# Softmax threshold and denominators as short sums on VectorE, and q and k loaded between their predecessors' copies

## The chip, the cores and the metric

The kernel runs on one core of a Trainium2 chip, in one launch. The metric is the device time of that core in microseconds (us). The core has TensorE (PE for the matmuls, PEld for its weight loads), VectorE (DVE), ScalarE (ACT), GpSimd (POOL) and SyncE (SP), which here issues nearly all DMAs.

## The reference

```python
def _attn_ref(q, k, v, tau):                  # q, k, v: 4 x 8 x 576 x 64, float32
    scores = scale * np.matmul(q, k.transpose(0, 1, 3, 2))
    thresh = np.max(scores, axis=-1, keepdims=True) - tau
    scores = np.where(scores >= thresh, scores, -1000000000.0)
    scores = scores - np.max(scores, axis=-1, keepdims=True)
    attn = np.exp(scores)
    attn = attn / (np.sum(attn, axis=-1, keepdims=True) + 1e-09)
    return np.matmul(attn, v)

def reference(...):
    x = attention(q, k, v, tau)               # to 2304 tokens x 512
    x = moe(x)     # a bias by modality, the best of 8 experts, relu between two matmuls, times the gate
    return moe2(x) # x @ w_in, h * tanh(softplus(h)), @ w_out
```

## The kernel before

The program has three stages one after the other on TensorE: attention (until about 347 us of the span), the 8 experts, and the dense last layer. The change is in the first.

**Attention.** Two heads of one batch element make a pair: 16 pairs. A pair's 576 rows of q are five units of 128 rows (the fifth has 64 rows of either head together). Below, unit (i, j) is unit j of pair i. `unit(u)` writes out one step of a pipeline by hand: scores of unit u, transposes of unit u - 1's probabilities, and products with v for unit u - 2. The order of instructions on each engine is that of the code; engines wait for one another by semaphores.

For each head x of a unit: `score` makes 128 x 576 negated scores in PSUM (tile `s`; two such tiles exist, so that the scores of a head wait until the tile's last user, two heads back, is done with it); `red` (L373, DVE) takes their minimum `mn`; `expo` has the threshold `th` = `mn` + `taus` made by a small instruction (L379, on POOL, in the first two units on DVE), and the exponential `e` (L381, ACT, with `mn` as its bias); `keep` (L391, DVE) sets to zero what lies beyond `th`, writes the probabilities `p`, and sums them into a column of the pair's 128 x 9 tile `rs`. `keep` is the tile `s`'s last user. At the end of unit (i, 1), `inverse` (L450 and L451, DVE) turns the denominators of the pair before into their reciprocals: plus 1e-9, then a reciprocal.

**q and k of the next pair.** In units 0 and 1 of a pair, `Prep` transposes q and k of the next one on TensorE: four transposes of `mq` or `mk` (L275) between the scores of the first and of the second head, and one of the last rows `rq` or `rk` (L291) later. ACT copies the results into `raw`, POOL splits `raw` into a high and a low part (`hi`, `lo` for q, `hik`, `lok` for k; L314 and L323), and SP copies the parts by DMA into the layouts that the scores read: `xq` (four DMAs of 128 KB, L332) and `xkh`, `xkl` (four DMAs each of 144 KB, L310). POOL's work on q stands in unit 1, that on k in unit 2. `Prep`'s own data is loaded a pair ahead: at the end of unit (i, 2), `load_qk` and `load_v` issue the loads of pair i + 2: `mq` and `mk` (256 KB each, in pieces of 256 bytes), `rq` and `rk` (64 KB each; of their 128 rows the first 64 are there too in `mq` and `mk`, and not used), and v. Further work (clearing `y_d`, the gate of the experts with stores to `x_d`, first expert weights) share the engines and the DMA queue in some pairs.

Of the kernel before, what the change touches and what calls it, by code (L numbers as in the profile page):

```python
# [9 lines left out]
F32 = mybir.dt.float32  # L10
# [10 lines left out]
P = 128  # L21
B, H, S, D = 4, 8, 576, 64
# [13 lines left out]
HK = S // 2  # L36
# [50 lines left out]
def chain_kernel(ctx: ExitStack, tc: tile.TileContext, q, k, v, tau, mid, w_gate, mbias, w1, w2, w_in, w_out, cst, out):  # L87
    nc = tc.nc
    ctx.enter_context(tc.manual_schedule())

    def pool(stack, name, bufs, **kw):
        return stack.enter_context(tc.tile_pool(name=name, bufs=bufs, reuse_waits="tile", **kw))
# [13 lines left out]
    def pa_tile(name):  # L106
        return ps_a.tile([P, 512], F32, tag="a", name=name)
# [23 lines left out]
    st_p = pool(ta, "st", 8)  # L131
# [6 lines left out]
    tau_b = att.tile([P, 1], F32, name="tau_b")  # L138
# [13 lines left out]
    PAIRS = [(b, g) for b in range(B) for g in range(NP)]  # L152
    ld = {}
    opd = {}
    res = {}

    def load_qk(i, n):
        b, g = PAIRS[i]
        h0 = 2 * g
        nm, src = (("q", q), ("k", k))[n]  # L160
        m = ld_p.tile([P, 4, 2, D], F32, name=f"m{nm}")
        r = ld_p.tile([P, 2, D], F32, name=f"r{nm}")
        ld[i, nm] = (m, r)
        parts = [
            lambda: nc.sync.dma_start(out=m, in_=src[b, h0:h0 + 2, 0:512, :].rearrange("h (p t) d -> p t h d", t=4)),
            lambda: nc.sync.dma_start(out=r, in_=src[b, h0:h0 + 2, 448:576, :].rearrange("h p d -> p h d"))]
        if i > 0:
            for x in parts:
                x()
        return parts  # L170

    def load_v(i):
        b, g = PAIRS[i]
# [6 lines left out]
        nc.sync.dma_start(out=vb[64:128, 128:192], in_=v[b, h0, 512:576, :])  # L180
        ld[i, "v"] = (m, vb)

    first = dict(zip("qk", (load_qk(0, 0), load_qk(0, 1))))
    first["i"] = [lambda: nc.sync.dma_start(out=ident, in_=cst[:, 0:P])]
    first["t"] = [lambda: nc.sync.dma_start(out=tau_b, in_=tau.to_broadcast([P, 1]))]
    for x in FIRST.split():
        first[x[0]][int(x[1:] or 0)]()
    load_qk(1, 0)
    load_qk(1, 1)

    neg = att.tile([P, 1], F32, name="neg")
    qsc = att.tile([P, 1], F32, name="qsc")
    taus = att.tile([P, 1], F32, name="taus")
# [153 lines left out]
    def score(i, j, x):  # L347
        o = opd[i]
        assert o["wait"] == 0 or i == 0 and j < NRAW
        s = ps_s.tile([P, 2, 512], F32, tag="s", name="s")  # L350
        res[i, j, x] = {"s": s}
        h = slice(64 * x, 64 * x + 64)
        for c in range(2):
            ks = slice(c * HK, (c + 1) * HK)
            kh = slice(k_off(x) + c * HK, k_off(x) + (c + 1) * HK)
            d = s[:, c, 0:HK]
            if i == 0 and j < NRAW:
                nc.tensor.matmul(d, lhsT=o["rawq"][h, 128 * j:128 * j + 128], rhs=o["rawk"][h, kh], start=True, stop=True)
            elif j < 4:
                qa = o["xq"][:, x, 128 * j:128 * j + 128]  # L360
                nc.tensor.matmul(d, lhsT=qa, rhs=o["xkh"][:, x, ks], start=True, stop=False)  # L361
                nc.tensor.matmul(d, lhsT=qa, rhs=o["xkl"][:, x, ks], start=False, stop=True)  # L362
            else:
                nc.tensor.matmul(d, lhsT=o["xm"][:, 0, :], rhs=o["hik"][:, kh], start=True, stop=False)
                nc.tensor.matmul(d, lhsT=o["xm"][:, 0, :], rhs=o["lok"][:, kh], start=False, stop=False)
                nc.tensor.matmul(d, lhsT=o["xm"][:, 1, :], rhs=o["hik"][:, kh], start=False, stop=True)

    def red(i, j, x):
        r = res[i, j, x]
        if x == 0:  # L370
            r["mn"], r["th"] = st_p.tile([P, 2], F32, name="mn"), st_p.tile([P, 2], F32, name="th")
        mn = res[i, j, 0]["mn"]
        nc.vector.tensor_reduce(out=mn[:, x:x + 1], in_=r["s"][:, :, 0:HK], op=ALU.min, axis=AX.XY)  # L373

    def expo(i, j, x):
        r = res[i, j, x]
        r["e"] = e_p.tile([P, 2, HK], F32, name="e")
        mt = res[i, j, 0]
        (nc.vector if (i, j) < (0, 2) else nc.gpsimd).tensor_scalar(  # L379
            out=mt["th"][:, x:x + 1], in0=mt["mn"][:, x:x + 1], scalar1=taus[:, 0:1], scalar2=0.0, op0=ALU.add, op1=ALU.add)  # L380
        nc.scalar.activation(out=r["e"], in_=r["s"][:, :, 0:HK], func=AF.Exp, scale=-1.0, bias=res[i, j, 0]["mn"][:, x:x + 1])  # L381

    def keep(i, j, x):
        r = res[i, j, x]
        if (j, x) == (0, 0):
            opd[i]["rs"] = rs_p.tile([P, 9], F32, name="rs")
        rs = opd[i]["rs"]
        if x == 0:
            r["pp"] = pp_p.tile([P, 2 * S], F32, name="p")
        p = res[i, j, 0]["pp"][:, x * S:(x + 1) * S].rearrange("p (a b) -> p a b", a=2)  # L390
        nc.vector.scalar_tensor_tensor(  # L391
            out=p, in0=r["s"][:, :, 0:HK], scalar=res[i, j, 0]["th"][:, x:x + 1], in1=r["e"],
            op0=ALU.is_le, op1=ALU.mult, accum_out=rs[:, 2 * j + x:2 * j + x + 1])
        r["p"] = res[i, j, 0]["pp"][:, x * (S + 64):x * (S + 64) + 512]

    def turn(i, j, x, cols):
# [49 lines left out]
        nc.scalar.copy(out=opd[b, "xt"][:, g, j * P:j * P + n], in_=a[:, 0:n])  # L446

    def inverse(i):
        rs = opd[i]["rs"]
        nc.vector.tensor_scalar(out=rs, in0=rs, scalar1=1e-9, scalar2=None, op0=ALU.add)  # L450
        nc.vector.reciprocal(out=rs, in_=rs)  # L451

    class Back(Piece):
# [573 lines left out]
    def unit(u):  # L1027
        i, j, n = at(u)
        i1, j1, n1 = at(u - 1)
        i2, j2, n2 = at(u - 2)  # L1030
        x, taken = None, False
        if n > 0 and j < 2 and i + 1 < len(PAIRS):
            x = Prep(i + 1, j)
        elif j == 3 and u >= 8:
            x = Back(u // 5 - 1)
        elif n > 0 and bg and hasattr(bg[0], "pe") and bg[0].ready():
            x, taken = bg.pop(0), True
        if n > 0:
# [59 lines left out]
    for n in PREP0:  # L1098
        x = Prep(0, n)
# [402 lines left out]
    with tc.If(cnt > i0):  # L1502
# [24 lines left out]
        with tc.For_i(b0, NT // 256) as k_:  # L1527
# [4 lines left out]
                out=y[1][:, :, 0:256].bitcast(F32),  # L1532
                in_=y_d.rearrange("k p (a c) -> k p a c", c=256)[:, :, bass.ds(k_, 1), :].rearrange("k p a c -> p k (a c)"))
# [60 lines left out]
```

## Time and profile before

| | |
|---|---|
| time before, median of 3 runs | 992.59 us (992.57 to 993.57) |
| time of the profiled execution | 996.13 us |
| its span, first to last instruction | 994.3 us |
| mean granted TensorE clock | 0.988 of full |
| busy in the span: PE, PEld, DVE, ACT, POOL | 94%, 79%, 82%, 52%, 67% |
| L373, minimum, DVE | 144 times, 750 ns |
| L391, `keep`, DVE | 144 times, 815 ns |
| L379, threshold, POOL | 140 times, 290 ns |
| `mq`, `mk`; `rq`, `rk` loads | 16 times each, 256 KB; 64 KB |

All times are microseconds from the span's start, durations of one instruction are nanoseconds where marked. The busy shares are means over three stages with different limits, so that a stage is read from its own windows and waits. A wait shown behind a row is the time in which that row's engine was idle before it, with what is taken to have ended it.

### The profile page before, as it was taken

Reading aid. Unit: us, or ns where it says so; the run is one execution under the profiler, and the core shown is the slowest. Engines: PE = TensorE matmul, PEld = TensorE weight load, DVE = VectorE, ACT = ScalarE, POOL = GpSimd, SP = SyncE. Lnnn points to the kernel's source line nnn. Section 1 sums busy time; section 2 is a strip of 40 time slices with the busy share of each in tenths; the row PEclk is TensorE's granted clock in tenths of the full one; section 3 lists DMA queues with packets and bytes.
Section 4 is the critical chain, followed back from the end, with each engine's and each line's share of the span. In section 5 each row is a group of like instructions: output and inputs, shape, how many; then the busy total and the mean of one; then the engine's idle time right before and its main releaser. Section 6 shows DMA issues by size and latency. Waiting matters only on the chain. (4 is left out here: it accounts for less than half of the span.)

```text
span 994.3 us, 17630 instructions
## 1 busy us (share of the span) xinstructions
PE 930.9 (94%) x6157; PEld 783.2 (79%) x6157; DVE 815.8 (82%) x1116; ACT 519.7 (52%) x1044; POOL 665.5 (67%) x771
## 2 busy tenths in 40 slices
PE   8899989998979997899999799999999999999994
PEld 5788888788868776688887788888888888888983
DVE  5677786687957768978876579999999999999992
ACT  4577777776768732366654643434344333433341
POOL 4354564455556364577876786887887888787883
PEclk9899999999999999999999999999999999999998
DMA  7678766646567053498899849010001100000000
GB/s 173 138 176 232 190 174 154 143 116 153 136 165 171 7 181 96 134 333 264 257 323 314 292 165 335 1 43 22 22 1 43 43 1 22 11 33 1 1 32 34
DMA packets 120526, 127.47 MB, mean 128 GB/s; under 512 B 54576, under 2 KB 83504, under 8 KB 119920
## 3 DMA queue, kind: packets, MB, share of 16 engines
q1 hardware_dynamic: 117472, 116.58, 40.8%
q0 software_dynamic: 2960, 9.70, 2.9%
q8 instruction: 51, 0.84, 0.3%
q14 instruction: 43, 0.35, 0.1%
HBM read 71.66 MB, written 27.33 MB: 100 GB/s over the span
## 5 line engine op out<-in xcount | busy, mean ns | idle before, releaser
L1298 DVE RECIPROCAL v<-v 128x512 f32<-128x512 f32 (+1 forms) x73 | 241.6, 3309 | 2.5
L373 DVE TENSOR_REDUCE mn<-s 128x1 f32<-128x576 f32 x144 | 106.3, 750 | 61.4 <-PE s L362 36.0
L381 ACT ACTIVATE e<-s,mn 128x576 f32<-128x576 f32 x144 | 105.1, 741 | 88.8 <-DVE mn L373 82.3
L379 POOL TENSOR_SCALAR th<-mn,taus 128x1 f32<-128x1 f32 x140 | 40.5, 290 | 147.5 <-DVE mn L373 134.5
L1292 POOL TENSOR_TENSOR u<-u,v 128x512 f32<-128x512 f32 (+1 forms) x73 | 93.1, 1276 | 64.4 <-ACT v L1291 63.0
L391 DVE SCALAR_TENSOR_TENSOR p<-s,th,e 128x576 f32<-128x576 f32 x144 | 115.2, 815 | 21.2 <-ACT e L381 9.3
L944 PE MATMUL h<-ybh,wil 128*128 128x512 f32 (+1 forms) x320 | 117.7, 368 | 0.0
L942 PE MATMUL h<-ybh,wih 128*128 128x512 f32 (+1 forms) x320 | 117.7, 368 | 0.0
L943 PE MATMUL h<-ybl,wih 128*128 128x512 f32 (+1 forms) x320 | 117.7, 368 | 0.0
L1321 PE MATMUL o<-wo,gh 128*128 128x512 f32 x288 | 112.8, 392 | 1.9 <-ACT gh L1305 1.5
L1297 DVE TENSOR_SCALAR v<-u 128x512 f32<-128x512 f32 (+1 forms) x73 | 109.5, 1500 | 5.6 <-POOL u L1292 3.7
L1323 PE MATMUL o<-wo,gl 128*128 128x512 f32 x288 | 112.7, 391 | 0.3
L1322 PE MATMUL o<-wo,gh 128*128 128x512 f32 x288 | 112.7, 391 | 0.0
L1289 ACT ACTIVATE u<-h 128x512 f32<-128x512 f32 (+1 forms) x73 | 43.2, 592 | 128.6 <-PE h L944 126.0
L1307 POOL TENSOR_TENSOR gl<-v,gh 128x512 fp32r<-128x512 f32 (+1 forms) x73 | 105.7, 1448 | 0.3 <-ACT gh L1305 0.3
L1305 ACT CAST gh<-v 128x512 fp32r<-128x512 f32 (+1 forms) x73 | 44.9, 615 | 111.3 <-DVE v L1303 111.3
L1299 POOL TENSOR_TENSOR u<-u,v 128x512 f32<-128x512 f32 (+1 forms) x73 | 93.3, 1278 | 7.7 <-DVE v L1298 7.7
L361 PE MATMUL s<-xkh,xq 128*128 128x288 f32 x248 | 81.2, 342 | 12.1 <-DVE p L391 10.1
L429 PE MATMUL av<-pt,mv 128*64 128x128 f32 (+1 forms) x1280 | 82.8, 272 | 0.0
L938 POOL TENSOR_TENSOR w0l<-w1r,w0h 128x512 fp32r<-128x512 f32 x39 | 50.7, 1300 | 47.4 <-ACT w0h L937 34.3
L401 PE MATMUL tp<-zident,p 128*128 128x128 f32 x576 | 79.3, 275 | 0.7 <-DVE p L391 0.4
L416 ACT COPY pt<-tp 128x512 f32<-128x512 f32 x144 | 78.4, 598 | 0.4 <-PE tp L401 0.4
(251 smaller groups left out, 2337.9 us busy)
## 6 DMA issues: line engine op xcount, KB each, us to landing
w1r<-in_moe_w SPq DMA_DIRECT2D x40, 256.0 KB
w2r<-in_moe_w SPq DMA_DIRECT2D x40, 256.0 KB
xkh<-hik SPq DMA_DIRECT2D x64, 144.0 KB
xkl<-lok SPq DMA_DIRECT2D x64, 144.0 KB
dr<-in_moe_w_in SPq DMA_DIRECT2D x16, 512.0 KB
dr<-in_moe_w_out SPq DMA_DIRECT2D x16, 512.0 KB
wo<-wo_d SPq DMA_DIRECT2D x14, 512.0 KB
y_d<-zero SPq DMA_DIRECT2D x8, 576.0 KB
```

The source lines that it names most:

```text
L373: nc.vector.tensor_reduce(out=mn[:, x:x + 1], in_=r["s"][:, :, 0:HK], op=ALU.min, axis=AX.XY)
L381: nc.scalar.activation(out=r["e"], in_=r["s"][:, :, 0:HK], func=AF.Exp, scale=-1.0, bias=res[i, j, 0]["mn"][:, x:x + 1])
L391: nc.vector.scalar_tensor_tensor(out=p, in0=r["s"][:, :, 0:HK], scalar=res[i, j, 0]["th"][:, x:x + 1], in1=r["e"], op0=ALU.is_le, op1=ALU. ...
L942: nc.tensor.matmul(o, lhsT=wh, rhs=xh, start=first, stop=False)
L943: nc.tensor.matmul(o, lhsT=wh, rhs=xl, start=False, stop=False)
L944: nc.tensor.matmul(o, lhsT=wl, rhs=xh, start=False, stop=last)
L1297: nc.vector.tensor_scalar(out=v_, in0=u, scalar1=WTOP, scalar2=2.0, op0=ALU.min, op1=ALU.add)
L1298: nc.vector.reciprocal(out=v_, in_=v_)
L1307: nc.gpsimd.tensor_tensor(out=l, in0=v_, in1=t.bitcast(F32), op=ALU.subtract)
L1321: nc.tensor.matmul(o, lhsT=gh[:, sl], rhs=wo[0, f_], start=f_ == 0, stop=False)
L1322: nc.tensor.matmul(o, lhsT=gh[:, sl], rhs=wo[1, f_], start=False, stop=False)
L1323: nc.tensor.matmul(o, lhsT=gl[:, sl], rhs=wo[0, f_], start=False, stop=f_ == NFO - 1)
```

## The change

The threshold is a sum over an axis of two: `red` writes the minimum into column 0 of a tile `mt` whose column 1 holds max(tau, 0) from the start, and the new `thresh` adds the two columns for both heads in one instruction on DVE (L389), ahead of the exponentials. The tile `mt` exists four times. L379 falls away on POOL. In the same way the denominators get their 1e-9 from a second column: `keep` sums into column 0 of a 128 x 9 x 2 tile that holds 1e-9 elsewhere, and `inverse` begins with a sum over that axis (L461) in place of the addition. The loads of q and k are parted: `mq` and `mk` of pair i + 2 are issued at the end of unit (i, 1), `rq` and `rk` at the end of unit (i, 2) as before, but only the 64 rows that are used, into tiles that are kept and whose other 64 rows are zeroed once.

```diff
     def load_qk(i, n):
-        r = ld_p.tile([P, 2, D], F32, name=f"r{nm}")
+        r = r_t[n][i % 2]
...
-            lambda: nc.sync.dma_start(out=r, in_=src[b, h0:h0 + 2, 448:576, :].rearrange("h p d -> p h d"))]
-        if i > 0:
-            for x in parts:
-                x()
-        return parts
+            lambda: nc.sync.dma_start(out=r[64:128], in_=src[b, h0:h0 + 2, 512:576, :].rearrange("h p d -> p h d"))]
...
+    r_t = [[att.tile([P, 2, D], F32, name=f"r{x}{i}") for i in range(2)] for x in "qk"]
+    for x in r_t:
+        for t in x:
+            nc.vector.memset(t[0:64], 0.0)
...
+    for i in range(3):
+        t = att.tile([P, 9, 2], F32, name=f"rs{i}")
+        nc.vector.memset(t, 1e-9)
+        rs_t.append(t)
...
+    for i in range(4):
+        t = att.tile([P, 2, 2], F32, name=f"mt{i}")
+        nc.vector.tensor_scalar(out=t[:, :, 1], in0=tau_b.to_broadcast([P, 2]), scalar1=0.0, scalar2=None, op0=ALU.max)
+        mt_t.append(t)
...
     def red(i, j, x):
-        nc.vector.tensor_reduce(out=mn[:, x:x + 1], in_=r["s"][:, :, 0:HK], op=ALU.min, axis=AX.XY)
+        nc.vector.tensor_reduce(out=mt[:, x, 0:1], in_=r["s"][:, :, 0:HK], op=ALU.min, axis=AX.XY)
+
+    def thresh(i, j, n):
+        r = res[i, j, 0]
+        nc.vector.tensor_reduce(out=r["th"][:, 0:n], in_=r["mt"][:, 0:n, :], op=ALU.add, axis=AX.X)
 
     def expo(i, j, x):
...
-        (nc.vector if (i, j) < (0, 2) else nc.gpsimd).tensor_scalar(
-            out=mt["th"][:, x:x + 1], in0=mt["mn"][:, x:x + 1], scalar1=taus[:, 0:1], scalar2=0.0, op0=ALU.add, op1=ALU.add)
...
     def inverse(i):
-        rs = opd[i]["rs"]
-        nc.vector.tensor_scalar(out=rs, in0=rs, scalar1=1e-9, scalar2=None, op0=ALU.add)
+        rs = opd[i]["rs"] = rs_p.tile([P, 9], F32, name="rs")
+        nc.vector.tensor_reduce(out=rs, in_=rs_t[i % 3], op=ALU.add, axis=AX.X)
         nc.vector.reciprocal(out=rs, in_=rs)
...
         if n > 0:
+            thresh(i, j, n)
             expo(i, j, 0)
...
+        if n > 0 and j == 1 and i + 2 < len(PAIRS):
+            late_loads = [load_qk(i + 2, z) for z in range(2)]
+            for z in late_loads:
+                z.pop(0)()
+            rest_loads[:] = [z[0] for z in late_loads]
         if n > 0 and j == 2 and i + 2 < len(PAIRS):
-            load_qk(i + 2, 0)
-            load_qk(i + 2, 1)
+            for z in rest_loads:
+                z()
             load_v(i + 2)
```

SP's queue in pair 6, from the copies of q to the loads of v, before the change (L632 and L634 are stores of the gate to `x_d`):

```order
L632 DMA x_d<-xo 128x2048
L332 DMA xq<-hi 64x512 x2
L332 DMA xq<-lo 64x512 x2
L310 DMA xkh<-hik 64x576 x4
L310 DMA xkl<-lok 64x576 x4
L634 DMA x_d<-xo 64x512
L165 DMA mq<-in_q 128x8x64
L166 DMA rq<-in_q 128x2x64
L165 DMA mk<-in_k 128x8x64
L166 DMA rk<-in_k 128x2x64
L176 DMA mv<-in_v 128x2x256
```

The same place of SP's queue now:

```order
L643 DMA x_d<-xo 128x2048
L343 DMA xq<-hi 64x512 x2
L343 DMA xq<-lo 64x512 x2
L165 DMA mq<-in_q 128x8x64
L165 DMA mk<-in_k 128x8x64
L321 DMA xkh<-hik 64x576 x4
L321 DMA xkl<-lok 64x576 x4
L645 DMA x_d<-xo 64x512
L166 DMA rq_137<-in_q 64x2x64
L166 DMA rk_139<-in_k 64x2x64
L172 DMA mv<-in_v 128x2x256
```

The loads of `mq` and `mk` moved ahead of the eight copies of k and ahead of the small store; `rq` and `rk` stayed behind them.

DVE around an `inverse`, from the minima of unit (1, 1) to those of unit (1, 2), before:

```order
L373 TENSOR_REDUCE mn<-s 128x1 x2
L391 SCALAR_TENSOR_TENSOR p,rs<-s,th,e 128x576 x2
L450 TENSOR_SCALAR rs<-rs 128x9
L451 RECIPROCAL rs<-rs 128x9
L373 TENSOR_REDUCE mn<-s 128x1 x2
```

The same place of DVE now:

```order
L384 TENSOR_REDUCE mt_192<-s 128x1 x2
L389 TENSOR_REDUCE th<-mt_192 128x2
L402 SCALAR_TENSOR_TENSOR p,rs_177<-s,th,e 128x576 x2
L461 TENSOR_REDUCE rs<-rs_175 128x9
L462 RECIPROCAL rs<-rs 128x9
L384 TENSOR_REDUCE mt_194<-s 128x1 x2
```

One instruction came in between the minima and `keep`, in every unit, and the first of the two of `inverse` is of another kind.

POOL in units 1 to 3 of a pair, before, from q's split to that of k:

```order
L314 TENSOR_SCALAR hi<-raw 128x576
L323 TENSOR_TENSOR lo<-raw,hi 128x576
L337 TENSOR_SCALAR xm_161<-hi 64x64 x2
L337 TENSOR_SCALAR xm_161<-lo 64x64 x2
L379 TENSOR_SCALAR th<-mn,taus 128x1 x2
L314 TENSOR_SCALAR hik<-raw 128x640
L323 TENSOR_TENSOR lok<-raw,hik 128x640
```

The same place of POOL now:

```order
L325 TENSOR_SCALAR hi<-raw 128x576
L334 TENSOR_TENSOR lo<-raw,hi 128x576
L348 TENSOR_SCALAR xm_165<-hi 64x64 x2
L348 TENSOR_SCALAR xm_165<-lo 64x64 x2
L325 TENSOR_SCALAR hik<-raw 128x640
L334 TENSOR_TENSOR lok<-raw,hik 128x640
```

The thresholds, which waited for DVE's minima of the unit, no longer stand ahead of the split of k (nor, in unit 1, ahead of that of q).

## Rows read from the trace of the kernel before

**Rows 1.** Window: PE, PEld, DVE, ACT, POOL busy us (instructions), clock, DMA share, GB/s.

```profile
0.00:347.00 347.00, 314.35 (x3199) 273.15 (x3200) 256.54 (x574) 245.17 (x577) 173.58 (x373) 0.98 0.62 152
```

**Rows 2.** Groups of TensorE's instructions, 0 to 350 us: busy, mean ns | idle before.

```profile
L361 PE MATMUL s<-xkh,xq 128*128 128x288 f32 x248 | 81.2, 342 | 12.1 <-DVE p L391 10.1 <-issue 1.1 <-PE av L407 0.9
...
L275 PE MATMUL ptq<-zident,mq 128*128 128x128 f32 x64 | 11.1, 300 | 12.6 <-DMA mq<-in_q 12.4
```

**Rows 3.** Timeline of TensorE, pair 7 into 8: start, us, instruction [idle before].

```profile
174.40 0.40 PE L361 MATMUL s<-xkh,xq 128*128 128x288 f32 x1
...
176.15 0.66 PE L275 MATMUL ptq<-zident,mq 128*128 128x128 f32 x4 [0.95 <-DMA mq<-in_q]
```

**Rows 4.** Timeline of SP's DMA issues in pair 7: start, us.

```profile
164.24 1.10 SPq L332 DMA_DIRECT2D xq<-lo  x2
166.86 2.39 SPq L310 DMA_DIRECT2D xkh<-hik  x4
...
171.88 0.66 SPq L165 DMA_DIRECT2D mq<-in_q  x1
```

**Rows 5.** Windows of the same stretch: copies of k, then mq.

```profile
167.50:173.25 5.75, 5.75 (x60) 5.25 (x60) 4.00 (x9) 4.13 (x12) 1.67 (x4) 1.00 0.89 206
173.25:174.65 1.40, 1.40 (x22) 1.23 (x23) 0.67 (x1) 1.40 (x3) 1.25 (x5) 1.00 0.82 185
```

**Rows 6.** Timeline of DVE, units (7, 0) to (7, 2).

```profile
157.99 0.81 DVE L391 SCALAR_TENSOR_TENSOR p<-s,th,e 128x576 f32<-128x576 f32 x1
...
160.93 0.76 DVE L373 TENSOR_REDUCE mn<-s 128x1 f32<-128x576 f32 x1 [0.22 <-PE s L362]
161.64 0.82 DVE L391 SCALAR_TENSOR_TENSOR p<-s,th,e 128x576 f32<-128x576 f32 x1
...
163.36 0.87 DVE L450 TENSOR_SCALAR rs<-rs 128x9 f32<-128x9 f32 x1
164.27 0.22 DVE L451 RECIPROCAL rs<-rs 128x9 f32<-128x9 f32 x1
164.40 1.36 DVE L373 TENSOR_REDUCE mn<-s 128x1 f32<-128x576 f32 x2
166.04 0.82 DVE L391 SCALAR_TENSOR_TENSOR p<-s,th,e 128x576 f32<-128x576 f32 x1 [0.28 <-ACT e L381]
```

**Rows 7.** Timeline of TensorE, the scores of units (7, 1) to (7, 3).

```profile
159.11 0.40 PE L361 MATMUL s<-xkh,xq 128*128 128x288 f32 x1
...
162.64 0.40 PE L361 MATMUL s<-xkh,xq 128*128 128x288 f32 x1
...
167.01 0.37 PE L361 MATMUL s<-xkh,xq 128*128 128x288 f32 x1 [0.64 <-DVE p L391]
```

**Rows 8.** Timeline of POOL in units (7, 1) and (7, 2).

```profile
162.79 1.42 POOL L323 TENSOR_TENSOR lo<-raw,hi 128x576 fp32r<-128x576 f32 x1
...
165.86 0.29 POOL L379 TENSOR_SCALAR th<-mn,taus 128x1 f32<-128x1 f32 x1 [0.15 <-DVE mn L373]
166.11 0.72 POOL L314 TENSOR_SCALAR hik<-raw 128x640 fp32r<-128x640 f32 x1
```

**Rows 9.** Timeline of ACT: the last copies into k's raw.

```profile
163.94 0.38 ACT L281 COPY raw<-av 128x64 f32<-128x64 f32 x2
```

**Rows 10.** Timeline of DVE in pair 10: a small sum on SBUF.

```profile
229.09 0.15 DVE L787 TENSOR_REDUCE t<-pre 128x1 f32<-128x8 f32 x1
```

**Rows 11.** Timeline of POOL at the same time.

```profile
228.50 1.56 POOL L323 TENSOR_TENSOR lok<-raw,hik 128x640 fp32r<-128x640 f32 x1
```

**Rows 12.** Timeline of TensorE at the end of pair 5's unit 3.

```profile
131.14 0.38 PE L364 MATMUL s<-hik,xm 128*128 128x288 f32 x1 [1.19 <-DVE p L391]
```

**Rows 13.** Timeline of TensorE in unit (13, 0).

```profile
280.21 0.37 PE L362 MATMUL s<-xkl,xq 128*128 128x288 f32 x1 [1.04 <-DMA xkl<-lok]
...
284.84 1.11 PE L275 MATMUL ptq<-zident,mq 128*128 128x128 f32 x4 [3.99 <-DMA mq<-in_q]
```

**Rows 14.** Window, columns as in rows 1, around that last wait.

```profile
284.30:287.70 3.40, 2.86 (x13) 2.85 (x14) 0.75 (x1) 0.00 (x0) 2.88 (x6) 0.50 0.45 119
```

More of the change, by code (lines that the diff above doesn't have):

```diff
@@ L161, in load_qk @@
         m = ld_p.tile([P, 4, 2, D], F32, name=f"m{nm}")
-        r = ld_p.tile([P, 2, D], F32, name=f"r{nm}")
+        r = r_t[n][i % 2]
         ld[i, nm] = (m, r)
-        parts = [
+        return [
             lambda: nc.sync.dma_start(out=m, in_=src[b, h0:h0 + 2, 0:512, :].rearrange("h (p t) d -> p t h d", t=4)),
-            lambda: nc.sync.dma_start(out=r, in_=src[b, h0:h0 + 2, 448:576, :].rearrange("h p d -> p h d"))]
-        if i > 0:
-            for x in parts:
-                x()
-        return parts
+            lambda: nc.sync.dma_start(out=r[64:128], in_=src[b, h0:h0 + 2, 512:576, :].rearrange("h p d -> p h d"))]
     def load_v(i):
@@ L187, in chain_kernel @@
         first[x[0]][int(x[1:] or 0)]()
-    load_qk(1, 0)
-    load_qk(1, 1)
+    for n in range(2):
+        for x in load_qk(1, n):
+            x()
     neg = att.tile([P, 1], F32, name="neg")
@@ L206, in chain_kernel @@
         vb_t.append(t)
+    mt_t, rs_t = [], []
+    for i in range(3):
+        t = att.tile([P, 9, 2], F32, name=f"rs{i}")
+        nc.vector.memset(t, 1e-9)
+        rs_t.append(t)
     mid_i = att.tile([P, B, 5, 2], I32, name="mid_i")
@@ L370, in red @@
         if x == 0:
-            r["mn"], r["th"] = st_p.tile([P, 2], F32, name="mn"), st_p.tile([P, 2], F32, name="th")
-        mn = res[i, j, 0]["mn"]
-        nc.vector.tensor_reduce(out=mn[:, x:x + 1], in_=r["s"][:, :, 0:HK], op=ALU.min, axis=AX.XY)
+            r["mt"], r["th"] = mt_t[(5 * i + j) % 4], st_p.tile([P, 2], F32, name="th")
+        mt = res[i, j, 0]["mt"]
+        nc.vector.tensor_reduce(out=mt[:, x, 0:1], in_=r["s"][:, :, 0:HK], op=ALU.min, axis=AX.XY)
+    def thresh(i, j, n):
+        r = res[i, j, 0]
+        nc.vector.tensor_reduce(out=r["th"][:, 0:n], in_=r["mt"][:, 0:n, :], op=ALU.add, axis=AX.X)
     def expo(i, j, x):
@@ L377, in expo @@
         r["e"] = e_p.tile([P, 2, HK], F32, name="e")
-        mt = res[i, j, 0]
-        (nc.vector if (i, j) < (0, 2) else nc.gpsimd).tensor_scalar(
-            out=mt["th"][:, x:x + 1], in0=mt["mn"][:, x:x + 1], scalar1=taus[:, 0:1], scalar2=0.0, op0=ALU.add, op1=ALU.add)
-        nc.scalar.activation(out=r["e"], in_=r["s"][:, :, 0:HK], func=AF.Exp, scale=-1.0, bias=res[i, j, 0]["mn"][:, x:x + 1])
+        nc.scalar.activation(out=r["e"], in_=r["s"][:, :, 0:HK], func=AF.Exp, scale=-1.0, bias=res[i, j, 0]["mt"][:, x, 0:1])
     def keep(i, j, x):
         r = res[i, j, x]
-        if (j, x) == (0, 0):
-            opd[i]["rs"] = rs_p.tile([P, 9], F32, name="rs")
-        rs = opd[i]["rs"]
+        rs = rs_t[i % 3]
         if x == 0:
@@ L392, in keep @@
             out=p, in0=r["s"][:, :, 0:HK], scalar=res[i, j, 0]["th"][:, x:x + 1], in1=r["e"],
-            op0=ALU.is_le, op1=ALU.mult, accum_out=rs[:, 2 * j + x:2 * j + x + 1])
+            op0=ALU.is_le, op1=ALU.mult, accum_out=rs[:, 2 * j + x, 0:1])
         r["p"] = res[i, j, 0]["pp"][:, x * (S + 64):x * (S + 64) + 512]
@@ L448, in inverse @@
     def inverse(i):
-        rs = opd[i]["rs"]
-        nc.vector.tensor_scalar(out=rs, in0=rs, scalar1=1e-9, scalar2=None, op0=ALU.add)
+        rs = opd[i]["rs"] = rs_p.tile([P, 9], F32, name="rs")
+        nc.vector.tensor_reduce(out=rs, in_=rs_t[i % 3], op=ALU.add, axis=AX.X)
         nc.vector.reciprocal(out=rs, in_=rs)
@@ L1012, in chain_kernel @@
     cleared = []
+    rest_loads = []
     def at(u):
```

## The prediction

> **What bounds the kernel now.** I read the windows first. Attention takes 347 of the 994 us of the span [rows 1], and TensorE is busy for 314 of them; the 33 us in which it idles there are the field on which this change plays, as everything behind attention hangs on TensorE's progress and should move with its end. The groups of TensorE's instructions then name the waits: 12.4 us before the transposes of `mq`, until its load has landed, and 10.1 us before the first scores of a unit, until `keep` has released the tile `s` [rows 2]. The second wait is not spread over the units: of its 18 occurrences 15 stand before a pair's unit 3, two steps behind an `inverse`, so I followed one, in pair 7, on all engines.
>
> **The wait for `mq`.** Scores start at 174.40 and the transposes behind them only at 176.15, idle 0.95 us [rows 3]. SP issued this load at 171.88, behind the eight copies of k, the first of which went out at 166.86 [rows 4]. The DMA rings were busy with the copies from 167.50 to 173.25 and with `mq` until 174.65 [rows 5]; TensorE saw it 1.5 us later. Nine pairs have such a wait, the longest 3.99 us [rows 13].
>
> **The wait for `keep`.** Behind the `keep` of (7, 1) L450, an addition on 128 x 9 numbers, takes 0.87 us from 163.36 on [rows 6]. It ends at 164.23, and POOL's `lo` ends at 164.21 [rows 8]: the addition stood still until POOL was done. The minima of (7, 2) start only at 164.40, `keep` at 166.04, and the scores of (7, 3) wait 0.64 us for it [rows 6, 7].
>
> **The change part by part.**
>
> *Loads moved.* `mq` and `mk` now stand behind `xq` (last issue ending at 165.34 [rows 4]) and ahead of the copies of k. Two transfers of at most 1.4 us each [rows 5] make about 2.5 us in front of the copies. What hides this is the earlier split of k: `raw` of k is ready at 164.32 [rows 9], but `hik` starts at 166.11, behind a threshold that waits for DVE's minima [rows 8]. Without thresholds on POOL it starts near 164.4, some 1.7 us earlier; q's split, behind two thresholds in the unit before, gains about as much, so `xq` is out of the rings before 165.1. `mq` and `mk` then fill 165.0 to 167.5, where the rings stood mostly idle, and the copies of k run from 167.5 to 173.2 as now. Seen 1.5 us later, the last is there at 174.7. The first head's scores begin at 174.40 now, would begin at 173.86 (0.54 earlier, below), and need six of the eight copies, there at 167.5 + 6/8 x 5.75 + 1.5 = 173.3. The second head's need all, and come behind the transposes of `mq`: TensorE ends the first head's at 176.15 - 0.95 = 175.20 now, at 174.66 then, and has the transposes (0.66 us with their pipeline [rows 3]) to do first. So the last copies arrive 0 to 0.6 us before they are wanted: **the wait for `mq` goes, and no other takes its place, but the margin is thin.** In five pairs the rings carry more (the first pair, stores of the gate, expert weights; pair 13's copies were 1.04 us late already [rows 13]), and there the copies come 2.5 - 1.7 = 0.8 us later and become the new wait: 5 x 0.8 = 4.0 us given back. [...] Sum of the loads: 12.4 - 4.0 + 1.7 = **10.1 us gained**; bounds 2 (copies late everywhere) to 17 (no wait left, every stretch behind one at full clock).
>
> *`rq` and `rk`* halve and land behind the copies, 128 small pieces each; they are wanted some 1 us after the second head's scores, at about 175.9, and are there by 174.7. Their cover is that 1 us. The memsets at the start stand before DVE's first real work; I cost them at nothing, since `rk`'s landing sets TensorE's start.
>
> *`inverse`.* The nearest row for the new sum is L787, 0.15 us, which began and ended while POOL's `lok` ran from 228.50 to 230.06 [rows 10, 11]: a small sum isn't held by POOL. I take 0.20 us for 128 x 9. The reciprocal then ends at 163.36 + 0.20 + 0.04 + 0.22 = 163.82, not 164.49.
>
> *`thresh`.* 0.15 us, and two dependences on DVE itself: L451, which needs L450's result, begins 0.04 us after its end, while the `keep` of 161.64, which needs no result of the minimum before it but that one's turn, began 0.05 us before its end, 160.93 + 0.76 [rows 6]. So `keep` starts 0.04 + 0.15 + 0.04 = 0.23 us after the second minimum, where it now starts at -0.05. The price is 0.28 us in a unit where DVE or a tie sets `keep`, and nothing where the exponential comes last by more than 0.23 us: the `keep` of 166.04 starts 0.28 us behind the minima, which end at 164.40 + 1.36 [rows 6]. Bounds: 0.15 from below; 0.87 from above, if it were held by POOL as L450 is.
> [...]
>
> *One pair, followed through.* Unit 0: `keep` ends at 158.80, the scores of (7, 1) start at 159.11 [rows 6, 7]; the shortest release seen is 0.15 (166.86 to 167.01), so 0.16 of the 0.28 is slack and **0.12 us is lost**. Unit 1: `keep` at 161.92, end 162.74, scores of (7, 2) at 162.89 in place of 162.64; the second `keep` waits for its own exponential in any case, so that its end hardly moves. Unit 2: minima at about 163.8 and, when the second head's scores are there, 164.5; `thresh` done at 165.46, `keep` at 165.50 in place of 166.04, scores of (7, 3) at 166.47 in place of 167.01: **0.54 us gained**, with TensorE free at 166.37. Units 3 and 4 have room, or wait for the exponential. Seven pairs show this 0.64 wait in full: 7 x 0.54 = 3.8 us. Of the 10.1 us [rows 2] that leaves 5.6; one wait in the last pair, 1.65 us, is gate work, and of the other 3.95 I take somewhat under half, 1.8: together **5.6 us gained**. Lost: 0.12 us in 13 pairs, 1.6, and in the six pairs with gate work, where DVE never rests and scores hang on its `keep` (1.19 us at 131.14 [rows 12]), about 0.35 us each (one `thresh` and part of another), 2.1: **3.7 us lost**.
>
> The sum is -10.1 - 5.6 + 3.7 = **-12.0 us**. On the profiled execution's 996.13 us that makes 984.1; that execution lies 3.5 us above the median of the runs shown, so the median should go from 992.6 to **980.6 us**, -1.2%.
>
> **The rivals.**
>
> *The copies of k take over.* If SP is held up in issuing the big loads, or the split of k gains less than 1.7 us, each of 13 pairs gives back another 0.8 us, as pair 13 already shows for its own [rows 13]: 10.4 us, leaving -1.6 us: 991.0; with half of it, 985.8. For it speaks the thin margin, against it the idle rings before 167.5. [...]
>
> *Slower: `thresh` holds `keep`.* If the delay is not 0.3 but d, a pair loses d - 0.16 in unit 0, d - 0.26 in unit 1 (through the second `keep`) and d - 0.27 in unit 2. Against gains of 15.7 us, 1.1 in each of 14 pairs, it decides from 3d - 0.69 = 1.1, d = 0.6, on. Held by POOL like L450, d would be 1.0 and the time some 17 us higher than before, 1009. L787's undelayed 0.15 us [rows 10, 11] speaks against it.
>
> *Nothing.* Attention ends earlier, but the expert stage starts on work that isn't moved (weights by DMA, the routing on DVE): 992.6. DVE's routing follows attention's end, so little speaks for it.
>
> *More.* All of the 12.4 us goes, and the half-clock stretches vanish, those of pairs 11 and 13 and part of an earlier one in pair 1: 17 us for the loads, -18.9 in all, 973.7.
>
> **How the numbers follow.** My case 60% (976 to 986, by the two bounds of how far `hik` gains and what the clock gives), copies take over 17%, more 10%, slower 7%, nothing 6%. The range is to leave out two tenths at most: it goes from 973.5, just below "more", to 990.5, which takes in two thirds of the second case. Of that case a third falls within 0.2% (2 us, about what a measurement of this kernel can tell). Faster: 60 + 10 + 12 = 82; the same: 6 + 5 = 11 less 2 for a small loss = 9; slower: 7 + 2 = 9.
>
> **What would show it.** After: L275's wait for `mq` gone from TensorE's groups; the first 256-byte load issued before the copies of k; `hik` within 0.2 us of ACT's last copy; the sum in `inverse` at 0.2 us in every pair; the wait for `keep` down from 10.1 to about 6 us, now spread over first units; `keep` 0.23 us behind the second minimum. I am wrong if L362 waits for `xkl` in most pairs, if the sum takes more than 0.3 us, or if attention ends before 337 us or after 345.

## The result, and the profile after

| | before | after |
|---|---|---|
| median, us | 993.08 (992.57 to 993.78, 4 runs) | 981.76 (979.95 to 983.6, 4 runs) |
| profiled execution, us | 996.13 | 983.6 |
| its span, us | 994.3 | 981.5 |

The ratio is 0.9878, with a 95% interval from 0.9859 to 0.9898: 1.2% faster, where 980.6 us and -1.2% were forecast. The window of attention, up to the start of the transposes of the last unit's probabilities (333.44 us, 346.64 before), answers to [rows 1]; its columns are the same. Before up to the same event, then after:

```profile
0.00:346.64 346.64, 313.99 (x3196) 272.80 (x3196) 256.21 (x573) 244.85 (x576) 173.30 (x372) 0.98 0.62 152
```
```profile
0.00:333.44 333.44, 308.76 (x3197) 270.57 (x3197) 260.80 (x659) 246.51 (x577) 135.67 (x235) 0.99 0.61 155
```

The kernel before had 313.99 us of TensorE's work in 346.64. So attention is 13.2 us shorter: TensorE idles 8.0 us less (24.68 against 32.65), and its work takes 5.2 us less. Behind attention the span has 648.1 us left against 647.7: nothing was won or lost there. Of the 5.2 us, some 3.1 are half of the work in two stretches of 3.4 us at half clock, 3.40 and 2.86 us (the second is [rows 14]), which this execution doesn't have: from 210 us on to the end of attention its granted clock is 1.00 in the windows, 0.98 and 0.97 before. I have no row for the other 2.1. Where such a stretch falls changes from one execution to the next: a second one of the changed kernel (the changed kernel again, below) has one between 230 and 250 us (0.91 over 20 us is what some 3.5 us at half clock make) and one less near 30 us (0.91 against 0.83 from 25 to 45 us). The stretch of the kernel before that isn't in [rows 14], then that second execution:

```profile
239.90:243.30 3.40, 3.40 (x27) 2.79 (x25) 2.77 (x9) 1.79 (x3) 0.29 (x1) 0.50 0.28 87
```
```profile
230.00:250.00 20.00, 16.32 (x161) 14.84 (x161) 17.01 (x47) 12.96 (x30) 5.74 (x11) 0.91 0.54 132
```

TensorE's groups, 0 to 335 us, answer to [rows 2].

```profile
L372 PE MATMUL s<-xkh,xq 128*128 128x288 f32 x248 | 80.6, 340 | 15.8 <-DVE p L402 13.6 <-PE av L418 0.9 <-DMA xkh<-hik 0.6
...
L373 PE MATMUL s<-xkl,xq 128*128 128x288 f32 x248 | 70.4, 298 | 2.9 <-DMA xkl<-lok 2.9
...
L286 PE MATMUL ptq<-zident,mq 128*128 128x128 f32 x64 | 10.1, 282 | 0.0
```

The wait for `mq` is gone, 12.4 us. The wait for `keep`, which was to fall from 10.1 us to about 6, has risen to 13.6. The copies of k (`xkh`, `xkl`) are waited for 3.5 us, against 2.2 before:

```profile
L362 PE MATMUL s<-xkl,xq 128*128 128x288 f32 x248 | 70.2, 297 | 2.2 <-DMA xkl<-lok 2.2
```

Two errors of opposite sign stand in a total that fits.

Pair 7 again: POOL's `hik` [rows 8], then SP's issues [rows 4].

```profile
160.53 0.73 POOL L325 TENSOR_SCALAR hik<-raw 128x640 fp32r<-128x640 f32 x1 [0.87 <-DMA xq<-hi]
```
```profile
160.23 0.66 SPq L165 DMA_DIRECT2D mq<-in_q  x1
160.94 0.74 SPq L165 DMA_DIRECT2D mk<-in_k  x1
161.78 2.56 SPq L321 DMA_DIRECT2D xkh<-hik  x4
164.44 2.46 SPq L321 DMA_DIRECT2D xkl<-lok  x4
```

ACT's last copy into `raw` ends at 160.38 (160.01 + 0.37), and `hik` starts 0.15 us behind it; before, it was 1.79 us. The loads go out ahead of the copies.

VectorE in units (7, 0) to (7, 2) [rows 6], then TensorE's scores that wait there [rows 7].

```profile
153.19 0.76 DVE L384 TENSOR_REDUCE mt<-s 128x1 f32<-128x576 f32 x1 [0.22 <-PE s L373]
153.98 0.16 DVE L389 TENSOR_REDUCE th<-mt 128x2 f32<-128x4 f32 x1
154.24 0.82 DVE L402 SCALAR_TENSOR_TENSOR p<-s,th,e 128x576 f32<-128x576 f32 x1
...
159.53 0.17 DVE L461 TENSOR_REDUCE rs<-rs 128x9 f32<-128x18 f32 x1
159.73 0.22 DVE L462 RECIPROCAL rs<-rs 128x9 f32<-128x9 f32 x1
159.86 1.46 DVE L384 TENSOR_REDUCE mt<-s 128x1 f32<-128x576 f32 x2
```
```profile
155.21 0.37 PE L372 MATMUL s<-xkh,xq 128*128 128x288 f32 x1 [0.16 <-DVE p L402]
...
159.02 0.37 PE L372 MATMUL s<-xkh,xq 128*128 128x288 f32 x1 [0.24 <-DVE p L402]
...
162.59 0.37 PE L372 MATMUL s<-xkh,xq 128*128 128x288 f32 x1
```

The second minimum ends at 153.95 and `keep` starts at 154.24, 0.29 us later. The wait of 0.64 us before unit 3 is gone; in its place nine pairs have a wait of 0.16 us before unit 1, and fourteen one of 0.24 before unit 2.

### The profile page after: what moved, and what is told of

It reads as the page before. It is cut to its first block, busy times and chain, and to the rows that moved or that the text cites. A ratio compares the mean times of both kernels' runs of the same rounds, so it can differ in the third digit from the quotient of the medians.

```text
span 981.5 us, 17499 instructions
## 1 busy us (share of the span) xinstructions
PE 931.9 (95%) x6157; PEld 786.8 (80%) x6157; DVE 821.1 (84%) x1203; ACT 520.7 (53%) x1044; POOL 626.6 (64%) x631
## 4 chain that ended last, share of the span: by engine, by line
PE 69%; DVE 14%; issue 4%; DMA 4%; SPq 3%; POOL 2%; ACT 2%; POOLq 0%; DVEq 0%; ACTq 0%
PE h L953 8%; PE h L955 8%; PE h L954 8%; PE o L1339 6%; PE o L1341 6%; PE o L1340 6%; PE s L372 4%; PE av L440 4%; DVE mt L384 3%; PE tp L412 3%; DVE p L402 3%; PE s L373 3%; PE y L953 2%; PE y L954 2%; PE y L955 2%
## 5 line engine op out<-in xcount | busy, mean ns | idle before, releaser
L384 DVE TENSOR_REDUCE mt<-s 128x1 f32<-128x576 f32 x144 | 108.0, 753 | 48.9 <-PE s L373 32.0
L394 ACT ACTIVATE e<-s,mt 128x576 f32<-128x576 f32 x144 | 106.3, 742 | 74.5 <-DVE mt L384 72.3
L402 DVE SCALAR_TENSOR_TENSOR p<-s,th,e 128x576 f32<-128x576 f32 x144 | 112.4, 814 | 13.5 <-ACT e L394 8.2
L372 PE MATMUL s<-xkh,xq 128*128 128x288 f32 x248 | 80.6, 340 | 15.8 <-DVE p L402 13.6
L440 PEld LDWEIGHTS av<-pt,mv 128*64 128x64 f32 x1280 | 64.1, 138 | 13.6 <-issue 13.2
## 6 DMA issues: line engine op xcount, KB each, us to landing
wo<-wo_d SPq DMA_DIRECT2D x14, 512.0 KB, 10.1
```

Of the source, the lines that this page charges most:

```text
L384: nc.vector.tensor_reduce(out=mt[:, x, 0:1], in_=r["s"][:, :, 0:HK], op=ALU.min, axis=AX.XY)
L402: nc.vector.scalar_tensor_tensor(out=p, in0=r["s"][:, :, 0:HK], scalar=res[i, j, 0]["th"][:, x:x + 1], in1=r["e"], op0=ALU.is_le, op1=ALU. ...
L440: nc.tensor.matmul(a[64 * x:64 * x + 64, 0:n], lhsT=m[:, x, c, :], rhs=sl, start=(c == 0), stop=False)
```

## The experiments

All stand beside runs of the kernel before on the same chip; the kernel before, pooled, has a median of 993.6, 994.0 and 995.4 us in the three groups. The third group (POOL's thresholds kept, the sum twice, halved loads alone) ran on another chip than the first two, so ratios are what can be set side by side across groups. The short diffs are against the changed kernel.

| kernel | median, us | ratio to before (95%) | waits of TensorE in attention, us: `mq`; copies of k; `keep` |
|---|---|---|---|
| before (profile) | | | 12.4; 2.2; 12.9 |
| halved loads alone | 993.8 | 0.999 (0.9973 to 1.0006) | 12.2; 0.5; 12.9 |
| inverse alone | 991.76 | 0.9976 (0.9958 to 0.9994) | 11.1; 1.7; 8.6 |
| threshold alone | 984.03 | 0.9887 (0.9865 to 0.9908) | 4.3; 0.7; 16.2 |
| both sums, old loads | 983.3 | 0.9893 (0.9866 to 0.992) | 4.7; 0.3; 14.8 |
| loads alone | 987.47 | 0.9925 (0.9898 to 0.9951) | 0; 5.9; 16.1 |
| loads and inverse | 986.6 | 0.9918 (0.989 to 0.9945) | 0; 8.6; 8.9 |
| changed kernel again | 982.06 | 0.9866 (0.984 to 0.9893) | 0; 3.8; 16.2 |
| both sums, old loads, POOL's thresholds kept | 997.07 | 1.0012 (0.9994 to 1.003) | 13.0; 1.2; 13.9 |
| sum of the threshold twice | 980.5 | 0.9847 (0.9827 to 0.9867) | 0; 3.3; 16.4 |
| threshold head by head | 977.37 | 0.983 (0.98 to 0.9859) | 0; 5.0; 10.1 |
| head by head, old loads | 979.84 | 0.9841 (0.9814 to 0.9868) | 5.5; 1.2; 10.0 |

The last column is by TensorE's groups; that of `keep` adds the waits of the usual scores, of unit 4's and of the last transposes (10.1 + 2.4 + 0.4 before, 13.6 + 1.5 + 1.0 in the profile after). Head by head, the profile names the small sum between the two `keep` as what ended most of these waits; they are counted here too.

**Loads alone.** Threshold and addition as before.

```diff
-            thresh(i, j, n)
             expo(i, j, 0)
...
+        (nc.vector if (i, j) < (0, 2) else nc.gpsimd).tensor_scalar(
+            out=mt["th"][:, x:x + 1], in0=mt["mt"][:, x, 0:1], scalar1=taus[:, 0:1], scalar2=0.0, op0=ALU.add, op1=ALU.add)
...
-        nc.vector.tensor_reduce(out=rs, in_=rs_t[i % 3], op=ALU.add, axis=AX.X)
+        nc.vector.tensor_scalar(out=rs, in0=rs_t[i % 3][:, :, 0], scalar1=1e-9, scalar2=None, op0=ALU.add)
```

> The loads' move alone: thresholds on POOL and the addition in `inverse` as before, everything else as in the changed kernel. Theory (the early loads fit only because POOL has no threshold ahead of the split of k): `hik` starts behind the threshold again, some 1.2 us later than in the changed kernel (160.53 there in pair 7, second minimum at 161.32 plus 0.44), the copies of k move by 0.7 to 1.2 us, and the scores wait for `xkl` in most pairs, 0.4 to 1.2 us each; the wait for `mq` is gone. Of the 12.4 us and the 5 us of clock some 6 to 15 are given back: 984 to 992 us. Rival (the rings have room in any case, POOL's thresholds don't matter): no wait for `xkl` beyond the first pair's, 975 to 980 us, as the waits for `keep` stay at the 12.9 us of the kernel before and not at the 16.1 of the changed one.

987.47 us, 0.9925: in the theory's range, but not for its reason. The copies of k were waited for in pairs 1 and 13, and 0.28 us in pair 11, not in most pairs, so the early loads mostly found room even with the late split. Of the theory stays that the copies take more in those pairs, 5.9 us against 2.2. The waits for `keep` rose too, from 12.9 to 16.1 us, with no sum of the threshold on VectorE; one wait in pair 13 alone is 2.59 us, and there `keep` itself waits for a threshold in POOL's queue:

```profile
278.84 0.82 DVE L405 SCALAR_TENSOR_TENSOR p<-s,th,e 128x576 f32<-128x576 f32 x1 [2.72 <-POOL th L395]
```

**Both sums, loads at their old place.**

```diff
-        if n > 0 and j == 1 and i + 2 < len(PAIRS):
-            late_loads = [load_qk(i + 2, z) for z in range(2)]
...
         if n > 0 and j == 2 and i + 2 < len(PAIRS):
-            for z in rest_loads:
-                z()
+            for z in range(2):
+                for y in load_qk(i + 2, z):
+                    y()
```

> Threshold and denominators as sums on VectorE, but `mq` and `mk` loaded where they were, behind the copies of k. Theory: the waits for `keep` are those of the changed kernel (about 16 us against 12.9 before, 3 lost), while the split of k starts earlier and draws the copies of k and the loads behind them forward by about 1.2 us in the nine pairs that waited for `mq`: of 12.4 us some 4 to 6 remain. 985 to 990 us. Rival (POOL's relief does nothing for the copies, the loads' place does it all): the wait for `mq` stays at 12 us and the time is 994 to 997 us.

983.3 us, 0.9893: more than the theory had. TensorE's group for the transposes of `mq`:

```profile
L286 PE MATMUL ptq<-zident,mq 128*128 128x128 f32 x64 | 10.1, 282 | 4.7 <-DMA mq<-in_q 4.7
```

Without any load moved, 7.7 of the 12.4 us are gone, and most of the gain is there.

**Loads and inverse, threshold on POOL.** The first two pieces of the diff of loads alone.

> The changed kernel with the threshold on POOL again, per head, and no `thresh` on VectorE; loads early, `inverse` as a sum. Theory: two things against each other. The regular waits of 0.165 and 0.24 us for `keep` (5.7 us in 14 pairs) and part of the larger ones in gate pairs go; `hik` starts some 1.2 us later, and the scores wait for `xkl` by 0.4 to 1 us in most pairs (6 to 14 us): 980 to 990 us, with the wait for `xkl` above 6 us in total. Rival (the rings have room in any case): 972 to 976 us, faster than the changed kernel, with the wait for `xkl` at its 2.9 us.

986.6 us: in the theory's range, and the wait for the copies rose to 8.6 us, in five pairs. Bringing the threshold to VectorE is worth some 4.5 us even where the loads stand early.

**Threshold head by head.**

```diff
             red(i, j, 0)
+            thresh(i, j, 0)
...
-            thresh(i, j, n)
             expo(i, j, 0)
...
         if n > 1:
+            thresh(i, j, 1)
             keep(i, j, 1)
```

> The changed kernel with the threshold made head by head: the sum for the first head right behind the first minimum (in the 0.21 us in which VectorE waits for the second head's scores), that for the second head between the two `keep`. Theory (what costs is that `keep` of the first head starts 0.29 us behind the second minimum, where -0.05 would do): `keep` starts 0.05 us before the second minimum's end, the regular waits of 0.165 and 0.24 us vanish, 5.7 us gained; the second `keep` starts where it does now or up to 0.1 us later. 974 to 978 us. Rival (VectorE's total work sets the pace, or the second `keep` does): one more instruction of 0.16 us in each unit, no gain or up to 5 us slower, 981 to 987 us.

977.37 us, 0.983, the fastest kernel here; `thresh` now takes one head's columns. VectorE in its unit (7, 0):

```profile
149.97 0.15 DVE L389 TENSOR_REDUCE th<-mt 128x1 f32<-128x2 f32 x1
150.16 0.76 DVE L384 TENSOR_REDUCE mt<-s 128x1 f32<-128x576 f32 x1
150.83 0.81 DVE L402 SCALAR_TENSOR_TENSOR p<-s,th,e 128x576 f32<-128x576 f32 x1
...
151.56 0.15 DVE L389 TENSOR_REDUCE th<-mt 128x1 f32<-128x2 f32 x1
151.82 0.82 DVE L402 SCALAR_TENSOR_TENSOR p<-s,th,e 128x576 f32<-128x576 f32 x1
```

`keep` starts 0.09 us before the end of the second minimum (150.92), not 0.29 behind it, and no wait of 0.16 or 0.24 us is left; those that remain stand in pairs with gate work. VectorE does more in all and TensorE waits 6.1 us less: the place of the sum was the price, as the theory says.

**Inverse alone.** Threshold on POOL, loads at their old place, the sum in `inverse` kept.

> Only the denominators' sum of the change: thresholds on POOL, `mq` and `mk` loaded behind the copies of k, `inverse` with the sum on VectorE. Theory (the wait before unit 3 goes, but the time that TensorE wins there is mostly waited for again at the next load of `mq`, which stands behind copies that POOL's split sets): wait for `keep` down from 12.9 us to about 8.5, wait for `mq` up from 12.4 to 14 to 17; 988 to 993 us. Rival (the two waits are independent, as the prediction's sum has it): wait for `mq` stays at 12.4 us, 5.6 us gained, 987 to 988.5 us.

991.76 us: the time lies in the theory's range and above the rival's. The waits decide for the rival: `keep` down from 12.9 to 8.6 us, `mq` not up but at 11.1. Against halved loads alone the gain is 1.4 us by the two ratios (0.9976 and 0.999), too little for their intervals; the profiled executions, on two chips, differ by 5.5 (989.98 and 995.44). So the size of the gain in time stays open. Why `keep` comes earlier doesn't: the addition of the kernel before, then the sum here, and the sum of pair 7 beside POOL's `lo`:

```profile
L450 DVE TENSOR_SCALAR rs<-rs x16: 168/876/886, 42.9 to 346.6; 128x9 f32<-128x9 f32 x16
```
```profile
L464 DVE TENSOR_REDUCE rs<-rs x16: 164/168/174, 41.4 to 339.7; 128x9 f32<-128x18 f32 x16
```
```profile
160.30 0.17 DVE L464 TENSOR_REDUCE rs<-rs 128x9 f32<-128x18 f32 x1
```
```profile
159.72 1.42 POOL L334 TENSOR_TENSOR lo<-raw,hi 128x576 fp32r<-128x576 f32 x1
```

The three numbers behind `x16` are the shortest, the median and the longest in ns. The sum starts and ends while `lo` runs, here and in 13 other pairs, and isn't held.

**Threshold alone.** Loads and addition as before, one sum per unit on VectorE.

> Only the threshold of the change: one sum per unit on VectorE, none on POOL; `inverse` with the addition, `mq` and `mk` loaded behind the copies of k. Theory (the threshold's leaving POOL lets the split of k start earlier, which draws the copies of k and the loads behind them forward): wait for `mq` down from 12.4 to 5 us or less, half-clock stretches in attention fewer, wait for `keep` up by 4 to 6 us; 984 to 989 us. Rival (the prediction's step: the threshold by itself only costs, 3.7 us, and the early split pays only together with the early loads): wait for `mq` at 12 us, 995 to 998 us.

984.03 us, 0.9887, as the theory has it, but for the wait for `keep`, which rose by 3.3 us and not by 4 to 6. POOL's `hik` and SP's load in pair 7, then all additions of `inverse` (as above):

```profile
159.36 0.73 POOL L325 TENSOR_SCALAR hik<-raw 128x640 fp32r<-128x640 f32 x1 [0.84 <-POOL xm L348]
```
```profile
165.11 0.66 SPq L165 DMA_DIRECT2D mq<-in_q  x1
```
```profile
L461 DVE TENSOR_SCALAR rs<-rs x16: 166/168/424, 41.8 to 335.9; 128x9 f32<-128x9 f32 x16
```

`raw` is ready at 159.21 (ACT, 158.84 + 0.37). `hik` follows after 0.15 us, and `mq` is issued 5.90 us after `raw`, against 7.56 before (171.88 - 164.32 [rows 4, 9]); the wait of 0.95 us in this pair is gone with no load moved. And the old addition, 876 ns in the median before, now takes 168: POOL's `lo`, no longer behind a threshold, is done before it (in pair 7 `lo` ends at 157.40, and the addition starts at 158.36).

**Head by head, loads at their old place.** The diffs of both sums and of head by head together.

> The threshold made head by head, as in the split version, but with `mq` and `mk` loaded behind the copies of k as before the change. Theory (once POOL has no threshold ahead of the split of k, the place of the loads is worth next to nothing): within 2 us of the split version with early loads, 976 to 980 us, with a wait for `mq` of some 5 us in place of the first and last pairs' waits for the copies of k. Rival (the loads' place has a worth of its own, up to the predicted 10 us, that the version with sums alone hid): 982 to 988 us.

979.84 us, 2.5 us more than with early loads: near the theory, far from the rival. By the ratios the early loads are worth 1.1 us here (0.983, 0.9841) and 2.7 with the threshold in one sum (0.9866, 0.9893); the intervals of these pairs overlap.

**The changed kernel again.**

> The changed kernel once more, on the same chip as the versions with a part of it, so that they can be set against it. 980 to 984 us by either theory; what counts is its distance to the version with sums alone and old loads (983.3 beside a kernel before of 993.55): within 2 us if the place of the loads hardly matters, 5 us or more if it does.

982.06 us, 1.2 us less than with the old loads by the medians: within the 2 us of the theory.

**POOL's thresholds kept beside VectorE's.** To both sums with old loads the old thresholds are added on POOL.

```diff
+        if x == 0:
+            mt["tp"] = st_p.tile([P, 2], F32, name="tp")
+        (nc.vector if (i, j) < (0, 2) else nc.gpsimd).tensor_scalar(
+            out=mt["tp"][:, x:x + 1], in0=mt["mt"][:, x, 0:1], scalar1=taus[:, 0:1], scalar2=0.0, op0=ALU.add, op1=ALU.add)
```

> The version with both sums on VectorE and old loads, and on POOL the thresholds of before once more, at their old place, into a tile that nobody reads: `keep` takes VectorE's. Theory (what the change gains, it gains because POOL's split of k no longer stands behind a threshold that waits for VectorE's minima): `hik` starts behind that instruction again, the wait for `mq` goes from 4.7 us back to 8 to 12, and of the 10.7 us between the kernel before and the version with sums most is lost: 989 to 995 us, the waits for `keep` staying at 14 us or more. Rival (TensorE merely comes later to `mq`, because it now waits 0.4 us in each pair for `keep`; POOL's queue plays no part): wait for `mq` stays near 5 us, 983 to 985 us.

997.07 us, 1.0012: the whole gain is lost, 11.8 us by the two ratios, for instructions of which nothing reads the result. POOL in pair 7, then the group of `mq`:

```profile
160.58 0.29 POOL L397 TENSOR_SCALAR tp<-mt,taus 128x1 f32<-128x1 f32 x1 [0.68 <-DVE mt L384]
160.83 0.67 POOL L325 TENSOR_SCALAR hi<-raw 128x576 fp32r<-128x576 f32 x1
...
163.59 0.54 POOL L348 TENSOR_SCALAR xm<-lo 64x64 fp32r<-64x64 f32 x2
164.23 0.56 POOL L397 TENSOR_SCALAR tp<-mt,taus 128x1 f32<-128x1 f32 x2
164.75 0.73 POOL L325 TENSOR_SCALAR hik<-raw 128x640 fp32r<-128x640 f32 x1
```
```profile
L286 PE MATMUL ptq<-zident,mq 128*128 128x128 f32 x64 | 10.8, 294 | 13.1 <-DMA mq<-in_q 13.0
```

k's `raw` was ready at 163.11 (ACT, 162.74 + 0.37); `hik` starts 1.64 us later, and `mq` is waited for 13.0 us. About 1.0 of the 1.64 us comes by way of q: a threshold that waited for VectorE's minimum stands ahead of `hi`, which starts 1.94 us after q's `raw` (158.54 + 0.35), so that POOL is at q's parts until 164.13. The two thresholds right ahead of `hik` add the rest. This is the clearest of the runs: the thresholds on POOL, ahead of the splits, are the cause. A run with them behind the splits would have parted their place from their mere presence; there is none.

**The sum twice.**

```diff
+        r["tx"] = st_p.tile([P, 2], F32, name="tx")
+        nc.vector.tensor_reduce(out=r["tx"][:, 0:n], in_=r["mt"][:, 0:n, :], op=ALU.add, axis=AX.X)
         nc.vector.tensor_reduce(out=r["th"][:, 0:n], in_=r["mt"][:, 0:n, :], op=ALU.add, axis=AX.X)
```

> The changed kernel with the threshold's sum made twice on VectorE, the first time into a tile that nobody reads (0.16 us more between the second minimum and `keep`). Theory (the sum lies on the path of `keep`, and TensorE waits for `keep` in units 1 and 2 of each pair without slack): the waits of 0.165 and 0.24 us grow by 0.16 to 0.2 each, waits before unit 3 appear, and the gate's pairs add another 2 us: 987 to 992 us. Rival (VectorE has room; the regular waits have another cause): within 2 us of the changed kernel, 980 to 984 us.

980.5 us, no slower than the changed kernel: by its time the rival's. The dose was smaller than meant:

```profile
153.29 0.16 DVE L390 TENSOR_REDUCE tx<-mt 128x2 f32<-128x4 f32 x1
153.37 0.15 DVE L391 TENSOR_REDUCE th<-mt 128x2 f32<-128x4 f32 x1
153.62 0.82 DVE L404 SCALAR_TENSOR_TENSOR p<-s,th,e 128x576 f32<-128x576 f32 x1
```

The second sum, which doesn't need the first, starts 0.08 us after it. The regular waits grew by 0.07 us each (0.23 and 0.30 for 0.16 and 0.24), 1.6 us in all, but one wait of 2.45 us in a gate pair shrank to 1.00, so the sum of waits for `keep` stands at 16.4. Why that one shrank is open; as a dose the run is inconclusive.

**Halved loads alone.** Everything undone but the halved `rq` and `rk`.

> All parts undone but the halved loads of `rq` and `rk` with their zeroed tiles (and the two-column tiles, of which only one column is used): threshold on POOL, addition in `inverse`, loads at their old place. Theory: nothing hangs on them, 992 to 995 us, as the kernel before, with the wait for `mq` at 12 us. Rival (the loads of `rq` and `rk` share the rings with `mq` and `mk`, and half of them less lets `mk` and v land earlier): the wait for `mq` falls below 11 us, 988 to 991 us.

993.8 us, 0.999: nothing, as costed.

## Why the prediction was right, and where it was wrong

The total was right, and so was the mechanism that it names, `hik` freed from the threshold. It was booked at the wrong place, and the terms missed by amounts that cancel: that the total came out within 1.2 us is in good part luck.

**Loads moved, 10.1 us gained.** In the changed kernel the wait for `mq` goes in full, the copies of k give back 1.3 us and not 4.0 (3.5 against 2.2), and TensorE's work takes 5.2 us less, not 1.7: 16.3 us. The forecast's 1.7 us, a term for the clock, no run shows as such; what shows in its place are the two stretches at a granted clock of 0.50, which the profile after doesn't have, some 3.1 of the 5.2 us. And the rings, which the text calls mostly idle from 165.0 to 167.5, had a DMA share of 0.53 there before, 0.08 from 166.5 on. But the step "the wait for `mq` goes" failed in its cause. The text used `hik`'s 1.7 us as cover for the moved loads, and didn't ask what they do alone. With the loads behind the copies an earlier split draws the loads forward too: `mq` went out 1.66 us earlier against `raw` in pair 7, and 8.1 of the 12.4 us went with the threshold alone. Nor do the thresholds right ahead of `hik`, to which the text puts its delay, make all of it. POOL in pair 7 of the kernel before:

```profile
162.03 0.67 POOL L314 TENSOR_SCALAR hi<-raw 128x576 fp32r<-128x576 f32 x1
...
164.78 0.54 POOL L337 TENSOR_SCALAR xm<-lo 64x64 fp32r<-64x64 f32 x2
```

Of `hik`'s 1.79 us behind `raw` 1.00 is POOL at q's parts until 165.32, late because `hi` stood behind two thresholds of unit 1, and 0.79 are the thresholds of unit 2.

Six of the nine waits for `mq` before (1.92, 0.62, 0.74, 1.32, 0.95, 1.96, 0.11, 3.99 and 0.89 us) were shorter than 1.7 us; this could have been read before. Moving the loads removes the same wait another way: alone 0.9925, on top of the sums 1 to 3 us.

**`inverse`, 5.6 us gained.** The sum takes 0.165 to 0.173 us in every pair (0.20 forecast), and the wait before unit 3 goes. But that wait would have gone anyway: with the threshold off POOL the old addition takes 168 ns. In the kernel before 14 of the 16 additions start while `lo` runs, take 0.64 to 0.89 us and end 0.02 to 0.04 us behind it, in pair 7 at 164.23 behind 164.21 [rows 6, 8]; the two others take 0.17 and 0.24 us. The two terms were added where they overlap: both sums together are not measurably faster than the threshold alone (0.9893, 0.9887). Only with thresholds on POOL does the changed `inverse` shorten the waits for `keep`, by 4.3 us alone; and alone it takes 0.2% (0.1 to 0.4%) off the kernel before, where 5.6 us, 0.6%, were booked.

**`thresh`, 3.7 us lost.** The price per unit was nearly right: `keep` starts 0.29 us behind the minimum (153.95 to 154.24), forecast 0.23; 0.03 of it lie before the sum, 0.16 are the sum, 0.10 lie behind it. What was mis-sized is how often it counts. The text lost 0.12 us in unit 0 of 13 pairs, and let the later scores of unit 1 (its own 0.25 us) be absorbed. They are not: 0.16 us in nine pairs and 0.24 in fourteen are 4.8 us, and taking the sum out of that path saved 6.1 us of waits, gate pairs included. With `inverse` together the prediction had 1.9 us gained on these waits; measured are 3.2 lost (12.9 to 16.2). The price of the sum by itself is what head by head shows, not this balance: loads alone has 16.1 us too, with no such sum on VectorE.

Sum: 16.3 - 3.2 = 13.1, beside 13.2 measured in attention and 12.0 forecast. The forecast sign "wrong if attention ends before 337" was badly set: its own sum ends attention at 347 - 12 = 335. **Halved loads** were rightly costed at nothing.

**The rivals.** The copies took over in single pairs only, 1.3 us. `thresh` held by POOL: no, 157 ns in the mean of its 80 instructions. *Nothing*: no, behind attention the span kept its length. *More*: its term for the loads (17 us) was nearly met by the measured 16.3; the waits for `keep` kept the total from it.

## What to carry to other kernels

A tiny instruction that waits for another engine, placed ahead of long work in a queue, can cost what stands behind it (11.8 us here, with POOL's thresholds kept): take it off and see what all of the queue's work releases. Before adding the gains of several edits, ask what each does to the same wait alone; here the threshold's move and the loads' move removed the same wait for `mq`, the threshold's move and the new `inverse` the same wait for `keep`, and the sum was right only because other errors had the other sign. A small instruction between a producer and a consumer goes where its engine waits anyway: the head-by-head threshold was worth another 4.7 us by the medians (982.06 to 977.37) and 3.6 by the two ratios, whose intervals overlap.

## What was not expected of the hardware

Here a sum over an axis of two on VectorE does the addition's work and isn't held by POOL's `lo`: 168 ns in the median beside it (inverse alone), where the addition took 876. And two small sums of 0.16 us on VectorE that don't need each other start 0.08 us apart (153.29 and 153.37), while `keep`, which needs the second, starts 0.25 us after it. So here the shown length of such an instruction is not its price: between the two independent ones it is half of that (0.08 of 0.16 us), ahead of the dependent `keep` 0.1 us more (0.25 for 0.15).
